# H3 sequence layer with a gated GLU, forward and backward: 128-channel key and value loads, a shorter sine table, and LN scaling and bf16 evacuations assigned to other engines

## The chip, the cores and the metric

One core of a Trainium2 chip. The metric is the device time of one execution in microseconds (us); runs are told by their median. The engines are named as the profile names them: PE multiplies matrices and transposes through them, DVE and ACT are the vector and the scalar engine, which also copy ("evacuate") PE's results from PSUM to SBUF, POOL issues one DMA queue and does small work, SP only issues DMAs (its own queue, in order).

## The reference

S = 2048 tokens, D = 512 channels, F = 1376, everything bf16. The kernel computes the output of the layer and, from `grad_out`, the gradients of nine of its inputs.

```
def _fwd_reference(A_q, A_k, A_v, A_shift_k, A_ssm_k, A_ssm_D, B_x, B_w_gate, B_w_up, B_w_down):
    xn = layernorm(A_q)
    k_shift = sum_t pad(A_k)[:, t:t+S] * A_shift_k[:, 3-t]      # four-tap causal convolution
    kv = k_shift * A_v
    y = irfft(rfft(kv, 2S) * rfft(A_ssm_k, 2S))[:, :S] + kv * A_ssm_D
    s = xn * y
    h = sigmoid(xn @ B_w_gate) * (xn @ B_w_up)
    return A_q + s * silu(h @ B_w_down)
# and the vector-Jacobian product with grad_out for q, k, v, shift_k, ssm_k, ssm_D, w_gate, w_up, w_down
```

## The kernel before

Nothing is emitted as it is written. Every `nc.<engine>.<op>` call is recorded by `Rec`, `Rec.order` (lines 348 to 504) gives each record a place by a list schedule with modelled costs (`cost`, `dcost`), and `emit` (line 506) issues the instructions in that order, which is why each instruction of the profile carries line 512. Each engine then runs its own list strictly in that order and waits on semaphores. An evacuation written as `nc.evac` (line 237) may go to ACT or DVE; the planner chooses (lines 414 to 420). So a changed cost or a changed program order moves instructions on all engines, but the order is fixed when the program is built.

The work has two stages around the change.

*FFT stage* (lines 766 to 1055, about the first 155 us). Four generators are merged by `run_streams` (line 1053):

- `strG` takes nine token tiles of 128 through `f_gen` (line 719): LN of a tile (`f_ln`, `f_ln2`: statistics on DVE, the power on POOL, then the scaling), its transpose (`f_xt`: PE with an evacuation, or a DMA transpose for some tiles), 88 matmuls with the gate and up weights, a sigmoid on ACT and a product on DVE (called `hT` below) for each of three blocks, and stores of `hT` and the sigmoid.
- `strV` does the four-tap convolution of the key with `A_shift_k` and the product with the value on DVE, per group of 128 channels (`GW`): eight TENSOR_TENSOR of 128x2048, 32 in all, and then the first FFT step on PE. Its loads are `ld_k` and `ld_v`, 256 channels each, so two groups share one load. The result of the convolution goes to DRAM (`ksh_d`) and its buffer `acc` is single.
- `strK` transforms the filter `A_ssm_k`: transposes (`k_t`), first step, then per quarter `flip` (eight PE transposes, a bf16 evacuation of 1024) and `step3` (f32 evacuation of 1024). Two SP DMAs swap the halves of each result (`slab<-slab`, 128 KB).
- `strX` flips and transforms the value side, multiplies both and goes back (`inv3`, `inv1`).

The FFT runs as matmuls with a sine table `Cf`, made at the start by `gen_fft_consts` (line 542): in four parts, integer products, masks to 13 bits, and one ACT sine of 1024 for cosine and sine together. The program order at the start is the loads of lines 812 to 824 on SP (filter, two token tiles, weights in three chunks, then key and value), the shift-filter broadcast `skb`, `k_t(0)`, and then the table with LN pieces between its yields (lines 850 to 860).

*Second stage* (line 1410 on): GLU down projection, all backward parts. Its instructions come after those of the FFT stage on each engine and need the results of that stage.

Transposes, flips and `k_t` write bf16 PSUM tiles; steps 1 and 3 and the inverse steps write f32 ones.

Of the kernel before, what the change touches and what calls it, by code (L numbers as in the profile page):

```python
# [16 lines left out]
P = 128  # L17
# [6 lines left out]
NJ = 16  # L24
# [132 lines left out]
class Op:  # L157
    __slots__ = ("n", "alts", "deps", "succ", "wait", "ready", "dma", "tiles", "done", "fin", "eng", "soft")

# [11 lines left out]
class Rec:  # L171
# [65 lines left out]
    def evac(self, dst, src, n):  # L237
        self.add([("scalar", "copy", (dst, src), {}), ("vector", "tensor_copy", (dst, src), {})])

# [48 lines left out]
    def cost(self, alt):  # L288

        eng, meth, a, k = alt  # L290
        out = k["out"] if "out" in k else a[0]
        n = self.size(out)
        if eng == "tensor":
            c = max(n, 128) / 2400 + 0.0025
            if out.ap.ap[0][1] <= 32 and len(out.ap.ap) > 2:
                c = 0.024
            return c, c + 0.163
        aps = [v for v in list(a) + list(k.values()) if isinstance(v, (PT, bass.AP))]
        big = [v for v in aps if self.size(v) >= n / 2]
        if eng == "scalar":  # L300
            ins = [v for v in big if v is not out]
            c = 0.045 + n * 0.84e-3
            if not any(isinstance(v, PT) for v in ins):
                c += 0.06 + (0.33e-3 * n if any(esize(v.dtype) == 4 for v in ins) else 0.0)
            return c, c + 0.11
        if eng == "vector":
            ps = any(isinstance(v, PT) for v in big)
            wide = any(esize(v.ap.dtype if isinstance(v, PT) else v.dtype) == 4 for v in big)
            rate, more = 960, 0.0
            if meth in ("tensor_copy", "tensor_scalar", "tensor_single_scalar", "tensor_scalar_add", "memset"):  # L310
                rate = 1920 if (wide and not ps) or (ps and not wide) else 960 if ps else 3840
                more = 0.11 if meth == "tensor_scalar" and n > 1000 else 0.0
            elif meth == "tensor_tensor" and not ps and not wide:
                rate = 1920
            if meth == "transpose":
                rate = 480
            if meth == "bn_stats":
                n, more = self.size(a[1]), 0.06
            elif meth == "scalar_tensor_tensor" and n > 100:
                more = 0.14  # L320
            c = 0.068 + n / rate + more
            return c, c + 0.085
        if "alu" in meth or meth == "tensor_tensor":
            return max(0.55, 0.2 + n * 2.1e-3), max(0.6, 0.25 + n * 2.1e-3)
        return 0.1 + n / 1000, 0.2 + n / 1000
# [22 lines left out]
    def order(self):  # L348
# [55 lines left out]
        while ndone < len(ops):  # L404
            best = None
            for e in self.ENGS:
# [135 lines left out]
def gen_fft_consts(nc, ar, negpi, Cf, TB):  # L542
    nc.vector.memset(negpi, -math.pi)
    sc = 2 * math.pi / 8192
# [9 lines left out]
    nc.gpsimd.iota(b, pattern=[[2, 128]], base=1, channel_multiplier=0)  # L554
    m = tmp([16, 128], i32)
    mc = tmp([2, 16, 128], i32)
# [54 lines left out]
    tri = tmp([5, 128], f32)  # L611
    nc.scalar.activation(tri, an, ACT.Sin, bias=negpi, scale=2 * math.pi / 16)
    nc.vector.tensor_tensor(TB[:, 0], tri[:, 0], mask[:, 0], ALU.mult)
# [11 lines left out]
def kernel_impl(ctx, tc, A_q, A_k, A_v, A_shift_k, A_ssm_k, A_ssm_D, B_x, B_w_gate, B_w_up, B_w_down,  # L625
# [29 lines left out]
    ident = Ring(ar, [P]).ap  # L655
    negpi = Ring(ar, [1], f32).ap
    TB = Ring(ar, [5, 128]).ap
# [133 lines left out]
    def ld_k(cp):  # L791
        c0, c1 = cp * 256, (cp + 1) * 256
        kh = kh_r.next()
# [5 lines left out]
    def ld_v(cp):  # L799
        vg = vg_r.next()  # L800
        nc.sync.dma_start(vg, vC[:, :, cp * 256:(cp + 1) * 256])
        stA["vg", cp] = vg
# [45 lines left out]
    for _ in k_t(0):  # L848
        pass
    consts = gen_fft_consts(nc, ar, negpi, Cf, TB)  # L850
    next(consts)
# [137 lines left out]
    def strV():  # L989
        for cg in range(NG):  # L990
            kh, vg = stA["kh", cg // 2], stA["vg", cg // 2]
            lc = (cg % 2) * GW
            c0, c1 = cg * GW, (cg + 1) * GW
            acc = acc_r.next()
            for lag in (3, 2, 1, 0):
                src = kh[:, 3 - lag: 3 - lag + NJ, lc:lc + GW]
                skl = skb[:, lag:lag + 1, c0:c1].to_broadcast([P, NJ, GW])
# [523 lines left out]
```

## Time and profile before

| what | value |
|---|---|
| median of 5 runs | 529.74 us (528.41 to 535.64) |
| the profiled execution: its own time | 530.13 us |
| its span, first to last instruction | 528.4 us |
| PE busy | 494.5 us, 94% of the span |
| DVE busy | 403.5 us, 76% |
| ACT busy | 342.5 us, 65% |
| POOL busy | 124.2 us, 24% |
| DMA moved | 113.19 MB, 214 GB/s on average |

Part 2 of the page cuts the span into 40 slices of 13.2 us and gives the busy share of each engine as one digit, so the FFT stage is the first twelve digits. The table of stretches gives, for a stretch of time, each engine's busy microseconds with the number of instructions in brackets, then the granted PE clock, the busy share of the DMA engines and the rate in GB/s. The groups by form name output, input, shapes and types, then the count, the busy sum and the mean ns of one instruction, then the idle time just before them and who ended it. The timeline lists instructions in order: start, duration, engine, operation, and in square brackets the idle time before it with the engine that ended it.

### The profile page before, as it was taken

Reading aid. Unit: us, or ns where it says so; the run is one execution under the profiler, and the core shown is the slowest. Engines: PE = TensorE matmul, PEld = TensorE weight load, DVE = VectorE, ACT = ScalarE, POOL = GpSimd, SP = SyncE. Lnnn points to the kernel's source line nnn. Section 1 sums busy time; section 2 is a strip of 40 time slices with the busy share of each in tenths; the row PEclk is TensorE's granted clock in tenths of the full one; section 3 lists DMA queues with packets and bytes.
Section 4 is the critical chain, followed back from the end, with each engine's and each line's share of the span. In section 5 each row is a group of like instructions: output and inputs, shape, how many; then the busy total and the mean of one; then the engine's idle time right before and its main releaser. Section 6 shows DMA issues by size and latency. Waiting matters only on the chain.

```text
span 528.4 us, 13550 instructions
## 1 busy us (share of the span) xinstructions
PE 494.5 (94%) x5429; PEld 349.4 (66%) x5429; DVE 403.5 (76%) x777; ACT 342.5 (65%) x455; POOL 124.2 (24%) x241
## 2 busy tenths in 40 slices
PE   4697899999999999999999999999999999998996
PEld 2686787898887676577775556644676755765643
DVE  7859999975749989978789999636758678773744
ACT  6899999999874345344443443326879968776621
POOL 5152533444513413424153221010000000000000
PEclk9899999999999999999999999999999999999999
DMA  8977796878999755647399946989898889999983
GB/s 258 258 226 267 240 336 203 265 238 244 225 197 216 165 154 147 207 118 194 109 253 244 205 137 176 224 249 255 188 255 220 204 261 213 253 182 241 210 213 117
DMA packets 173713, 113.19 MB, mean 214 GB/s; under 512 B 114487, under 2 KB 158161, under 8 KB 173394
## 3 DMA queue, kind: packets, MB, share of 16 engines
q1 hardware_dynamic: 162016, 78.43, 62.2%
q0 software_dynamic: 11104, 33.89, 21.0%
q8 instruction: 42, 0.69, 0.6%
q14 instruction: 21, 0.17, 0.1%
q10 hardware_dynamic: 530, 0.01, 0.1%
HBM read 37.65 MB, written 45.72 MB: 158 GB/s over the span
## 4 chain that ended last, share of the span: by engine, by line
PE 51%; DVE 21%; ACT 10%; issue 8%; DMA 6%; POOL 3%; DVEq 0%; POOLq 0%; ACTq 0%
PE psum L512 51%; DVE slab L512 21%; ACT slab L512 10%; DMA ksh_d<-slab 2%; DMA slab<-in_A_q_dram 1%; DMA KK_d<-slab 1%; DMA out_dram<-slab 1%; POOL slab L512 1%; POOL hF_d L512 1%; DMA Ci_d<-slab 1%; POOL KK_d L512 1%; POOL ksh_d L512 0%; POOL sF_d L512 0%; DVEq L512 0%; POOLq L512 0%
## 5 line engine op out<-in xcount | busy, mean ns | idle before, releaser
L512 PE MATMUL psum<-slab 128*128 128x128 bf16 (+4 forms) x5429 | 494.5, 255 | 29.0 <-ACT slab L512 17.1
L512 PEld LDWEIGHTS <-slab 128*128 128x128 bf16 (+2 forms) x5429 | 349.4, 99 | 173.8 <-issue 24.2
L512 DVE TENSOR_TENSOR slab<-slab 128x512 bf16<-128x512 bf16 (+6 forms) x472 | 268.6, 608 | 48.3 <-ACT slab L512 24.5
L512 ACT CAST slab<-psum 128x1024 bf16<-128x1024 f32 (+3 forms) x270 | 219.5, 861 | 98.2 <-PE psum L512 70.8
L512 ACT ACTIVATE slab<-psum 128x512 bf16<-128x512 f32 (+2 forms) x80 | 55.5, 694 | 45.5 <-PE psum L512 43.0
L512 ACT ACTIVATE slab<-slab 128x512 bf16<-128x512 bf16 (+2 forms) x53 | 42.1, 799 | 22.1 <-DVE slab L512 21.5
L512 ACT COPY slab<-psum 128x1024 bf16<-128x1024 bf16 (+1 forms) x49 | 46.9, 998 | 13.9 <-PE psum L512 13.9
L512 POOL DMA_DIRECT2D out_dram<-slab x32 | 17.5, 545 | 102.9 <-DVE slab L512 102.9
L512 DVE CAST slab<-psum 128x1024 bf16<-128x1024 f32 (+2 forms) x24 | 27.0, 1126 | 16.5 <-PE psum L512 13.8
L512 DVE TENSOR_TENSOR slab<-psum,slab 128x512 bf16<-128x512 f32 (+2 forms) x47 | 29.3, 626 | 11.9 <-ACT slab L512 7.2
L512 DVE SCALAR_TENSOR_TENSOR slab<-slab 128x512 bf16<-128x512 bf16 (+2 forms) x64 | 28.1, 439 | 7.9 <-POOL slab L512 5.7
L512 POOL DMA_DIRECT2D hF_d<-slab x48 | 26.0, 545 | 31.4 <-DVE slab L512 31.2
L512 POOL MEMSET slab<- 128x128 bf16 (+3 forms) x11 | 4.3, 400 | 118.0 <-PE psum L512 117.6
L512 DVE SCALAR_TENSOR_TENSOR slab<-psum,slab 128x512 bf16<-128x512 f32 x16 | 11.0, 688 | 21.0 <-PE psum L512 21.0
L512 POOL DMA_DIRECT2D KK_d<-slab x32 | 17.5, 546 | 21.7 <-ACT slab L512 18.5
L512 POOL DMA_DIRECT2D slab<-in_A_q_dram x29 | 16.2, 557 | 24.1 <-ACT slab L512 18.7
L512 DVE TENSOR_SCALAR slab<-slab 128x1 f32<-128x1 f32 (+9 forms) x54 | 16.4, 324 | 2.2 <-ACT slab L512 1.2
L512 DVE STREAM_TRANSPOSE slab<-slab 128x1024 f32<-128x1024 f32 x8 | 14.3, 1826 | 4.3 <-ACT slab L512 4.3
L512 POOL DMA_DIRECT2D slab<-hF_d x18 | 9.7, 542 | 10.8 <-PE psum L512 10.0
L512 DVE BATCH_NORM_STATS2 slab<-slab 128x6 f32<-128x512 bf16 x16 | 11.0, 687 | 1.4 <-DMA slab<-in_A_q_dram 1.4
L512 POOL TENSOR_TENSOR slab<-slab 128x1 f32<-128x1 f32 x16 | 9.8, 613 | 9.5 <-DVE slab L512 9.3
L512 POOL DMA_DIRECT2D slab<-in_grad_out_dram x16 | 8.6, 540 | 6.0 <-DMA out_dram<-slab 4.6
(20 smaller groups left out, 32.8 us busy)
## 6 DMA issues: line engine op xcount, KB each, us to landing
KK_d<-slab POOLq DMA_DIRECT2D x32, 256.0 KB, 4.3
slab<-KK_d SPq DMA_DIRECT2D x16, 512.0 KB, 4.4
slab<-in_A_v_dram SPq DMA_DIRECT2D x4, 1024.0 KB, 9.4
hF_d<-slab POOLq DMA_DIRECT2D x32, 128.0 KB, 3.8
slab<-slab SPq DMA_DIRECT2D x32, 128.0 KB, 4.7
out_dram<-slab POOLq DMA_DIRECT2D x32, 128.0 KB, 2.7
uF_d<-slab SPq DMA_DIRECT2D x32, 128.0 KB, 2.3
gF_d<-slab SPq DMA_DIRECT2D x32, 128.0 KB, 2.3
```

Of the source, the lines that this page charges most:

```text
L512: getattr(getattr(self.nc, eng), meth)(*[place(v) for v in a], **{x: place(v) for x, v in k.items()})
```

## The change

Key and value are loaded per 128 channels (eight loads each way instead of four, buffers of half the size, two of each), the first group ahead of the weights on SP's queue; the second group and the filter's second part are loaded at the end of the start-up. Of the table's four integer products three go to POOL; the two masks and an add become one shift pair and an absolute value (`-1 * x max x`), and cosine and sine are two ACT sines of 512 each. In the FFT stage LN's scaling is one DVE instruction with two per-partition scalars instead of a DVE product and an ACT instruction. The transposes of tiles 2 and 3 in the sequence go through PE instead of DMA. In the planner, evacuations of 2-byte PSUM tiles carry a bias of 0.3 us towards DVE, and the cost of 4-byte SBUF operations on DVE is set higher.

```
     def evac(self, dst, src, n):
-        self.add([("scalar", "copy", (dst, src), {}), ("vector", "tensor_copy", (dst, src), {})])
+        op = self.add([("scalar", "copy", (dst, src), {}), ("vector", "tensor_copy", (dst, src), {})])
+        op.bias = 0.3 if esize(src.ap.dtype) == 2 else 0
...
-                rate = 1920 if (wide and not ps) or (ps and not wide) else 960 if ps else 3840
+                rate = 1200 if wide and not ps else 1920 if ps and not wide else 960 if ps else 3840
...
-                    o = min(either, key=lambda o: (max(o.ready, free[e]), o.n))
+                    sg = 1.0 if e == "scalar" else -1.0
+                    o = min(either, key=lambda o: (max(o.ready, free[e]) + sg * o.bias, o.n))
                     s = (max(o.ready, free[e]), o.n, e, 1)
-                    late = free["scalar"] - s[0]
+                    late = free["scalar"] - s[0] + o.bias
...
+    nc.vector.memset(negpi[:, 1:2], math.pi / 2)
...
+    yield
+    m = tmp([4, 4, 128], i32)
+    mc = tmp([4, 2, 4, 128], i32)
+    for h in range(4):
+        eng = nc.gpsimd if h > 0 else nc.vector
+        eng.tensor_tensor(out=m[:, h], in0=a[:, 4 * h:4 * h + 4, None].to_broadcast([P, 4, 128]),
+                          in1=b[:, None, :].to_broadcast([P, 4, 128]), op=ALU.mult)
     for h in range(4):
         js = slice(4 * h, 4 * h + 4)
-        if h in (1, 2):
+        if h > 1:
             yield
-        nc.vector.tensor_tensor(m[:, js], a[:, js, None].to_broadcast([P, 4, 128]),
-                                b[:, None, :].to_broadcast([P, 4, 128]), ALU.mult)
-        nc.vector.tensor_single_scalar(mc[:, 0, js], m[:, js], 6144, ALU.add)
-        nc.vector.tensor_single_scalar(mc[:, 0, js], mc[:, 0, js], 8191, ALU.bitwise_and)
-        nc.vector.tensor_single_scalar(mc[:, 1, js], m[:, js], 8191, ALU.bitwise_and)
-        nc.scalar.activation(Cf[:, :, js], mc[:, :, js], ACT.Sin, bias=negpi, scale=sc)
+        nc.vector.tensor_scalar(mc[:, h, 1], m[:, h], 19, 19, ALU.logical_shift_left, ALU.arith_shift_right)
+        nc.scalar.activation(Cf[:, 1, js], mc[:, h, 1], ACT.Sin, scale=-sc)
+        nc.vector.scalar_tensor_tensor(mc[:, h, 0], mc[:, h, 1], -1, mc[:, h, 1], ALU.mult, ALU.max)
+        nc.scalar.activation(Cf[:, 0, js], mc[:, h, 0], ACT.Sin, bias=negpi[:, 1:2], scale=-sc)
...
     def f_ln2(i):
         xj, st = T[i]["xq"], T[i]["st"]
+        if PS["wide"]:
+            nc.vector.tensor_scalar(xnA[:, i, :], xj, st[:, 6:7], rstd_all[:, i:i + 1], ALU.subtract, ALU.mult)
+            return
...
     def f_xt(i):
-        if POS[i] > 1 and not 8 < POS[i] < 12:
+        if POS[i] > 3 and not 8 < POS[i] < 12:
...
-    kh_r = Ring(ar, [NJ + 3, 2 * GW])
-    vg_r = Ring(ar, [NJ, 2 * GW])
+    kh_r = Ring(ar, [NJ + 3, GW], n=2)
+    vg_r = Ring(ar, [NJ, GW], n=2)
...
     def ld_k(cp):
-        c0, c1 = cp * 256, (cp + 1) * 256
+        c0, c1 = cp * GW, (cp + 1) * GW
...
+    ld_k(0)
+    ld_v(0)
     ld_w(0, 512)
     ld_x(SEQ[2])
     ld_w(512, 1024)
     ld_w(1024, F)
-    ld_k(0)
-    ld_v(0)
...
+    consts = gen_fft_consts(nc, ar, negpi, Cf, TB)
+    next(consts)
     make_identity(nc, ident)
...
-    consts = gen_fft_consts(nc, ar, negpi, Cf, TB)
     next(consts)
     f_ln(SEQ[0])
     next(consts)
     f_xt(SEQ[0])
     f_ln(SEQ[1])
     next(consts)
+    ld_KT(1)
+    ld_k(1)
+    ld_v(1)
...
-            if cg + 1 < NG:
+            if 0 < cg < NG - 1:
                 ld_KT(cg + 1)
...
             kvt = kvt_r.next()
-            nc.vector.tensor_tensor(kvt, acc, vg[:, :, lc:lc + GW], ALU.mult)
-            if cg == 1:
-                ld_k(1)
-                ld_v(1)
+            nc.vector.tensor_tensor(kvt, acc, vg, ALU.mult)
+            if cg + 2 < NG:
+                ld_k(cg + 2)
+                ld_v(cg + 2)
```

More of the change, by code (lines that the diff above doesn't have):

```diff
@@ L157 @@
 class Op:
-    __slots__ = ("n", "alts", "deps", "succ", "wait", "ready", "dma", "tiles", "done", "fin", "eng", "soft")
+    __slots__ = ("n", "alts", "deps", "succ", "wait", "ready", "dma", "tiles", "done", "fin", "eng", "soft", "bias")
 class EngRec:
@@ L542, in gen_fft_consts @@
 def gen_fft_consts(nc, ar, negpi, Cf, TB):
-    nc.vector.memset(negpi, -math.pi)
+    nc.vector.memset(negpi[:, 0:1], -math.pi)
+    nc.vector.memset(negpi[:, 1:2], math.pi / 2)
     sc = 2 * math.pi / 8192
@@ L554, in gen_fft_consts @@
     nc.gpsimd.iota(b, pattern=[[2, 128]], base=1, channel_multiplier=0)
-    m = tmp([16, 128], i32)
-    mc = tmp([2, 16, 128], i32)
+    yield
[5 more added lines that the diff above has]
+                          in1=b[:, None, :].to_broadcast([P, 4, 128]), op=ALU.mult)
     for h in range(4):
         js = slice(4 * h, 4 * h + 4)
-        if h in (1, 2):
+        if h > 1:
             yield
-        nc.vector.tensor_tensor(m[:, js], a[:, js, None].to_broadcast([P, 4, 128]),
-                                b[:, None, :].to_broadcast([P, 4, 128]), ALU.mult)
-        nc.vector.tensor_single_scalar(mc[:, 0, js], m[:, js], 6144, ALU.add)
-        nc.vector.tensor_single_scalar(mc[:, 0, js], mc[:, 0, js], 8191, ALU.bitwise_and)
-        nc.vector.tensor_single_scalar(mc[:, 1, js], m[:, js], 8191, ALU.bitwise_and)
-        nc.scalar.activation(Cf[:, :, js], mc[:, :, js], ACT.Sin, bias=negpi, scale=sc)
+        nc.vector.tensor_scalar(mc[:, h, 1], m[:, h], 19, 19, ALU.logical_shift_left, ALU.arith_shift_right)
+        nc.scalar.activation(Cf[:, 1, js], mc[:, h, 1], ACT.Sin, scale=-sc)
+        nc.vector.scalar_tensor_tensor(mc[:, h, 0], mc[:, h, 1], -1, mc[:, h, 1], ALU.mult, ALU.max)
+        nc.scalar.activation(Cf[:, 0, js], mc[:, h, 0], ACT.Sin, bias=negpi[:, 1:2], scale=-sc)
     yield
@@ L611, in gen_fft_consts @@
     tri = tmp([5, 128], f32)
-    nc.scalar.activation(tri, an, ACT.Sin, bias=negpi, scale=2 * math.pi / 16)
+    nc.scalar.activation(tri, an, ACT.Sin, bias=negpi[:, 0:1], scale=2 * math.pi / 16)
     nc.vector.tensor_tensor(TB[:, 0], tri[:, 0], mask[:, 0], ALU.mult)
@@ L655, in kernel_impl @@
     ident = Ring(ar, [P]).ap
-    negpi = Ring(ar, [1], f32).ap
+    negpi = Ring(ar, [2], f32).ap
     TB = Ring(ar, [5, 128]).ap
@@ L800, in ld_v @@
         vg = vg_r.next()
-        nc.sync.dma_start(vg, vC[:, :, cp * 256:(cp + 1) * 256])
+        nc.sync.dma_start(vg, vC[:, :, cp * GW:(cp + 1) * GW])
         stA["vg", cp] = vg
@@ L990, in strV @@
         for cg in range(NG):
-            kh, vg = stA["kh", cg // 2], stA["vg", cg // 2]
-            lc = (cg % 2) * GW
+            kh, vg = stA["kh", cg], stA["vg", cg]
             c0, c1 = cg * GW, (cg + 1) * GW
@@ L995, in strV @@
             for lag in (3, 2, 1, 0):
-                src = kh[:, 3 - lag: 3 - lag + NJ, lc:lc + GW]
+                src = kh[:, 3 - lag: 3 - lag + NJ]
                 skl = skb[:, lag:lag + 1, c0:c1].to_broadcast([P, NJ, GW])
```

## The prediction, made before the changed kernel ran

> **What bounds the kernel now.** I read the busy shares in slices first, to find the stage where PE isn't full.
>
> ```profile
> PE   4697899999999999999999999999999999998996
> DVE  7859999975749989978789999636758678773744
> ACT  6899999999874345344443443326879968776621
> ```
>
> After the twelfth slice PE is at 9 nearly throughout. In slices 3 to 10 ACT is at 9, and DVE nearly so in 4 to 8. The built order of the changed kernel ends, on every engine, with the same long run of instructions as before (on PE the last 6995 rows, on DVE 540, on ACT 284), so all that is new lies in the FFT stage. The stretches cut it at the first and the last instruction of the convolution, and at 158.5 us, where PE's long unbroken run starts:
>
> ```profile
> 0.00:34.70 34.70, 22.35 (x277) 18.98 (x278) 22.90 (x72) 28.28 (x35) 14.96 (x35) 0.95 0.87 254
> 34.70:104.75 70.05, 61.86 (x923) 54.01 (x921) 65.92 (x89) 69.81 (x84) 27.75 (x50) 1.00 0.83 257
> 104.75:158.50 53.75, 52.06 (x809) 46.90 (x805) 33.41 (x62) 48.93 (x65) 21.82 (x43) 1.00 0.98 227
> 158.50:528.40 369.90, 358.26 (x3428) 229.53 (x3427) 281.26 (x558) 195.53 (x274) 59.71 (x113) 1.00 0.82 200
> ```
>
> Columns: length, then PE, weight loads, DVE, ACT, POOL, clock, DMA share, GB/s. In the second stretch ACT is busy 69.81 of 70.05 us and DVE 65.92: two full engines, PE waits on them. In the third PE is full (52.06 of 53.75). So the stage has a start, a DVE/ACT stretch and a PE stretch. What ends the start is seen in the timeline:
>
> ```profile
> 15.04 5.49 PE L512 MATMUL psum<-slab 128*128 128x128 bf16 x66 [2.32 <-ACT slab L512]
> 34.11 0.69 DVE L512 TENSOR_TENSOR slab<-psum,slab 128x512 bf16<-128x512 f32 x1 [1.62 <-ACT slab L512]
> 34.72 9.90 DVE L512 TENSOR_TENSOR slab<-slab 128x2048 bf16<-128x2048 bf16 x8
> ```
>
> The convolution stands on DVE behind five hT products, and the fifth, at 34.11, waited for a sigmoid on a full ACT. The same five products stand ahead of it in the new order.
>
> **The change, part by part.** Durations come from the groups by form:
>
> ```profile
> L512 ACT COPY slab<-psum 128x1024 bf16<-128x1024 bf16 x39 | 41.2, 1102 | 1.4 <-PE psum L512 1.4
> L512 ACT ACTIVATE slab<-slab 128x512 bf16<-128x512 bf16 x48 | 36.9, 771 | 19.3 <-DVE slab L512 18.7
> L512 ACT ACTIVATE slab<-slab 128x1024 bf16<-128x1024 int32 x4 | 4.5, 1140 | 2.6 <-DVE slab L512 2.6
> L512 DVE COPY slab<-psum 128x1024 bf16<-128x1024 bf16 x5 | 3.4, 688 | 1.5 <-ACT slab L512 0.8 <-PE psum L512 0.7
> L512 DVE CAST slab<-psum 128x1024 bf16<-128x1024 f32 x20 | 24.4, 1221 | 10.2 <-PE psum L512 7.5 <-DMA out_dram<-slab 2.1 <-ACT slab L512 0.4
> L512 DVE TENSOR_SCALAR slab<-slab 128x512 int32<-128x512 int32 x12 | 5.8, 515 | 1.4 <-ACT slab L512 1.2
> L512 DVE TENSOR_SCALAR slab<-slab 128x1408 bf16<-128x1408 bf16 x9 | 4.7, 523 | 0.1
> L512 DVE TENSOR_TENSOR slab<-slab 128x512 int32<-128x512 int32 x4 | 2.7, 683 | 1.3 <-POOL slab L512 1.3
> L512 DVE SCALAR_TENSOR_TENSOR slab<-slab 128x1 f32<-128x1 f32 x16 | 2.5, 154 | 5.7 <-POOL slab L512 5.7
> ```
>
> On ACT consecutive instructions overlap: in the timeline a 1024 evacuation starts 0.90 us after the one before it and an LN scaling holds the engine 0.72 (sigmoids 0.49 for 512, 0.38 for 384), so I count those spacings, row by row in the built order where I give ACT's work up to a point.
>
> *LN scaling, 11 tiles.* ACT loses 11 x 0.72 = 7.9 us. DVE gets 11 instructions of 512 in bf16. None is in the trace. Nearest is TENSOR_SCALAR 128x1408, 523 ns; with 128x1 at 154 ns the slope gives 154 + 512 x 0.262 = 288 ns. The upper end is the rate of BN_STATS on 512, 687 ns. I take 0.29: 3.2 us, less 11 x 0.154 = 1.7 for the product that goes, +1.5 (up to +5.9). DVE waited for POOL's power before, at that product, so no wait is new.
>
> *Evacuations.* By the built order eight bf16 ones of 1024 move from ACT to DVE, three f32 ones come back, and DVE has two more of 512, as tiles 2 and 3 now go through PE. ACT: -8 x 0.90 + 3 x 0.90 = -4.5. DVE: 8 x 0.688 - 3 x 1.221 + 2 x 0.425 = +2.7. PE gets eight transposes, 8 x 0.064 = 0.5 (the rate of its run of 192 in 12.26 us). SP loses two DMA transposes of about 1.3 us each.
>
> *Table.* DVE: 4 x 0.683 + 12 x 0.515 = 8.9 becomes 0.683 + 4 x 0.515 + 4 x 0.70 (the absolute value has two int32 inputs, as the product) = 5.5. ACT: one table load less (1.28), but eight sines of 512; 640 takes 828 ns and 1024 takes 1140, so 512 takes 724 by their slope, and 0.62 in spacing: 8 x 0.62 - 4 x 1.02 = +0.9.
>
> *Three products on POOL.* No row of before is near: POOL's 128x1 power takes 0.61 us, the lower end. The Trainium skill ("GPSIMD Engine Reference", 3.1 and 4.1) speaks against the move: it prices a two-input elementwise instruction at about 2.6 cycles an element at 1.2 GHz, an estimate of 1.1 us for 512, and advises VectorE. Twice that is my upper end. I take 1.1, 3.3 in all, from about 2.5 to 6 us. POOL's iotas stand behind, and DVE's small mask chain needs them only after 13 us; the first power before came at 10.15. With 2.2 each POOL would be free at 9, still in time. Hidden.
>
> *Loads.* Before the weights stand now 1.05 MB more. At the first stretch's 254 GB/s that is 4.1 us. The runs are 256 bytes instead of 512. These rows bear on it:
>
> ```profile
> slab<-in_A_ssm_k_dram SPq DMA_DIRECT2D x4, 512.0 KB, 6.1
> slab<-in_A_k_dram SPq DMA_DIRECT2D x2, 1024.0 KB, 9.3
> slab<-in_A_k_dram SPq DMA_DIRECT2D x4, 512.0 KB, 6.6
> ```
>
> The last line is this load, as the backward part already makes it: 0.5 us more than the filter, which has long runs and the same size. The Trainium skill ("DMA: Bandwidth & Descriptors", Specifications) says that transfers under 512 bytes miss line rate; if that halved it, 512 KB would land like 1024 KB, 2.7 us later, +5.4 for the pair ahead of the weights, and 8 x 2.7 = 22 over the stage. By the row it is +1.0 for the pair and 4 in all, on queues with a share of 0.83. I take the row. The last weights landed at 15.4 us (issued 6.84, 8.5 to landing); they will at 20.5 (rule: 25).
>
> *The start, summed.* The filter lands as before, so DVE reaches its k_t addition at 8.31. From there it has, ahead of the first token transpose's evacuation (now its own): two sets of LN statistics, 2 x (0.687 + 0.180 + 0.154) = 2.0; the last table part, 1.2; two scalings, 0.6; the mask chain, 3.2 between 15.04 and 18.2 in the trace, and tiny ones, 1.2; the evacuation, 0.4. That makes 16.9, so the gate matmuls start 2 us later than at 15.04. But the sines end near 15.3 (k_t's evacuations end at 11.56, then six x 0.62) instead of 18.4, so the 32 filter matmuls no longer share that run, and ACT has before the fifth sigmoid 17.5 us of work instead of 27.7, since flips, LN scalings and a table load went behind or away. PE then has 176 matmuls until the fifth hT: 176 x 0.064 = 11.3, to 28.2. With the product and latencies the convolution starts at 29.6 instead of 34.7: -5.1. Bounds: PE at the start's colder rate, 66 in 5.49 us, gives 31.6 plus 1.4, -1.7; no queueing behind the mask chain gives 26.5, -8.
>
> *The stretch.* In the new order DVE has between first and last convolution instruction 6 bf16 evacuations more, 3 f32 fewer, one statistics set fewer, one hT more, and 4 scalings for 4 products: 4.1 - 3.7 - 1.0 + 0.7 + 0.5 = +0.6. So DVE needs 65.9 + 0.6 = 66.5. ACT's work up to that point falls from 97.1 to 87.3, of which 66.7 are behind the start. PE has then done 1180 matmuls, 1172 before; about 950 fall in here, 950 x 0.067 = 63.7. Three engines near 65 don't interlock without loss; of 70.05 I take off 1.0 (0 to 3.5). DVE is the bound next, not ACT.
>
> *After it.* PE has the same work left and is full: 53.75, plus 0.5 for the transposes counted at the whole stage. Then the old list.
>
> Sum: -5.1 - 1.0 + 0.1 (the part of the transposes outside waits) = -6.0. The profiled execution took 530.13 us, 1.7 beside its span of 528.4, and would take 524.1. It is 0.39 above the median of the runs, 529.74, so I predict 523.7.
>
> **The rivals.**
>
> *ACT alone was the bound.* Its row of nines speaks for it. It sheds 7.9 + 4.5 + 1.28 - 0.9 = 12.8 us and the stage shrinks by 12: 517.7. Against it: DVE's 65.92 in the stretch doesn't shrink.
>
> *The gain is lost.* DVE's queue at the start decides: gate matmuls wait for an evacuation behind the mask chain, weights come later, and a cold PE starts the convolution near 34; the stretch stays at 70. Then -1: 529.
>
> *Slower, through SP's queue.* Groups 2 and 3 are loaded singly, each only once a convolution frees its buffer, and SP stands still meanwhile, with the half-swaps of the filter's transforms behind it. Before, the one such load held SP for 7.34 us (from 55.11). Two of them held so, each passed on whole to the products that stand on DVE among the convolution, cost 14.7: 529.74 - 6.0 + 14.7 = 538.4. It decides once SP is held longer than the swaps lead their products. Early this lead is some 20 us (30.4 to 53.4); against it too, DVE waited on swaps nowhere in this stage.
>
> **How the numbers follow.** Likeliest, -6: 0.52, own range 518 to 527. ACT alone: 0.20. Lost: 0.14. Slower: 0.14. About 1%, 5.3 us, is what a measurement of this kernel can tell, so faster means below 524.4: two thirds of the first case and all of the second, 0.56; same 0.30, the rest of the first and the third; slower 0.14. The range leaves out the slow case and the best end of the second: 514 to 531.
>
> **What would show it.** Right: first convolution instruction near 29.6, first sigmoid near 18 (20.72 before), the convolution's last end near 98.6, ACT below 97% in the stretch, PE's unbroken run starting near 152.5, scalings near 0.29 us. Wrong: a convolution start at 34 or later, a stretch over 71, DVE waits on `slab<-slab` or `in_A_k_dram` of microseconds, POOL products over 2.2 us, or a third stretch that keeps PE waiting on DMA, whose share there is already 0.98.

## The result and the profile after

The changed kernel takes 529.80 us (median of 44 runs), the kernel before 529.45 (79 runs): ratio 0.9993, 95% interval 0.9977 to 1.0009. The ratio leaves out the executions that lie over 1.5% above the fastest of their kernel (11 of the 44, two of them at 856 and 1799 us), so it is not the quotient of the two medians. The forecast was 523.7. The profiled execution of the changed kernel took 531.28 us, with a span of 529.5.

The slices first (PE, DVE, ACT, busy share in tenths):

```profile
PE   3889899999997999999999999999999999999996
DVE  8889989686758679978789999645758768883844
ACT  6689999788963344334443353234888968786621
```

PE is at 8 or 9 from the second slice on (before, from the fifth), and has a 7 in the thirteenth that was not there before. The stretches, cut at the same times as before (the last one is 0.6 us longer):

```profile
0.00:34.70 34.70, 23.81 (x287) 20.80 (x288) 28.99 (x72) 23.40 (x33) 20.27 (x41) 1.00 0.93 246
34.70:104.75 70.05, 63.57 (x937) 56.45 (x936) 63.79 (x86) 66.56 (x78) 28.69 (x49) 0.98 0.86 263
104.75:158.50 53.75, 53.49 (x819) 47.72 (x817) 37.51 (x70) 46.74 (x63) 22.38 (x44) 1.00 0.98 227
158.50:529.00 370.50, 356.85 (x3402) 227.85 (x3400) 278.66 (x552) 194.00 (x270) 59.03 (x112) 0.99 0.82 199
```

ACT has five nines in the first twelve slices, where it had eight: 23.40 us of work in the first stretch instead of 28.28, 66.56 in the second instead of 69.81. PE did more than before in each of the first three stretches (140.9 us up to 158.5, before 136.3), but in the last one it has 356.85 us of work where it had 358.26 in a shorter stretch, and the clock is 0.99 instead of 1.00. The timeline of the start shows where the convolution went (DVE; the fifth hT product, a product of one column between, then the convolution):

```profile
30.24 0.69 DVE L514 TENSOR_TENSOR slab<-psum,slab 128x512 bf16<-128x512 f32 x1 [0.20 <-PE psum L514]
30.85 6.13 DVE L514 TENSOR_TENSOR slab<-slab 128x2048 bf16<-128x2048 bf16 x5
```

It starts at 30.85 instead of 34.72, -3.9. I call the stage's end the first gate product of the second stage on DVE, which needs everything of the FFT stage behind it on PE: 156.32 before, 153.31 now, -3.0.

```profile
156.32 0.69 DVE L512 TENSOR_TENSOR slab<-psum,slab 128x512 bf16<-128x512 f32 x1 [3.14 <-ACT slab L512]
153.31 0.69 DVE L514 TENSOR_TENSOR slab<-psum,slab 128x512 bf16<-128x512 f32 x1 [3.45 <-ACT slab L514]
```

So the stage did become shorter. The work moved as it was built to: the groups by form, ACT's bf16 evacuations (39 before) and LN scalings (48 with those of the backward part), DVE's evacuations (5 bf16, 20 f32 before) and the new scalings.

```profile
L514 ACT COPY slab<-psum 128x1024 bf16<-128x1024 bf16 x31 | 33.2, 1108 | 4.3 <-PE psum L514 4.1
L514 ACT ACTIVATE slab<-slab 128x512 bf16<-128x512 bf16 x37 | 27.1, 735 | 19.2 <-DVE slab L514 18.7
L514 DVE CAST slab<-psum 128x1024 bf16<-128x1024 f32 x17 | 20.8, 1221 | 9.9 <-PE psum L514 8.6 <-ACT slab L514 1.1
L514 DVE COPY slab<-psum 128x1024 bf16<-128x1024 bf16 x13 | 8.8, 686 | 0.7 <-PE psum L514 0.5
L514 DVE TENSOR_SCALAR slab<-slab 128x512 bf16<-128x512 bf16 x11 | 5.6, 507 | 1.8 <-POOL slab L514 1.6
```

From the stage's end on, every engine has the list of before, and the gain is gone within 23 us. The timelines of PE, first the kernel before (from 160 us), then the changed one (from 150 us):

```profile
159.70 30.47 PE L512 MATMUL psum<-slab 128*128 128x512 bf16 x325
```

```profile
149.75 15.90 PE L514 MATMUL psum<-slab 128*128 128x512 bf16 x204
169.28 10.92 PE L514 MATMUL psum<-slab 128*128 128x512 bf16 x87 [3.63 <-DVE slab L514]
```

Before, PE ran on without a gap. Now it stands still for 3.63 us from 165.65, ahead of the input gradient of tile 0 (`x_gen(0)`: 11 matmuls of `duT` with the transposed up weights `wuT`, then 11 of `dgT` with `wgT`). DVE reads the sum at 175.81; before it did so at 173.85. A gain of 3.0 has become a loss of 2.0.

```profile
173.85 0.68 DVE L512 SCALAR_TENSOR_TENSOR slab<-psum,slab 128x512 bf16<-128x512 f32 x1
175.81 0.69 DVE L514 SCALAR_TENSOR_TENSOR slab<-psum,slab 128x512 bf16<-128x512 f32 x1 [4.89 <-PE psum L514]
```

The bracket names DVE, but DVE was through with its run of 16 products at 167.8, and in the kernel before PE passed this point while DVE was still in the same run (before first, then changed):

```profile
163.81 6.95 DVE L512 TENSOR_TENSOR slab<-slab 128x512 bf16<-128x512 bf16 x16
160.80 6.96 DVE L514 TENSOR_TENSOR slab<-slab 128x512 bf16<-128x512 bf16 x16
```

Each of the first eleven matmuls reads `wuT` over all its columns, so it needs all four transposes of the up weights, which SP issues last of twelve weight transposes. The view of these, in a window with the last two of the four, first before, then changed:

```profile
L512 SPq DMA_TRANSPOSE slab<-in_B_w_up_dram x2: 1802/2142/2483, 160.0 to 162.6; - x2
DMA to landing us min/median/max: 4.6/5.1/5.5
```

```profile
L514 SPq DMA_TRANSPOSE slab<-in_B_w_up_dram x2: 2241/2292/2342, 157.6 to 159.9; - x2
DMA to landing us min/median/max: 9.2/9.2/9.2
```

In the changed kernel the last was issued at 159.9 and landed 9.2 later, at 169.1: PE starts at 169.28. Before, the last of the four was issued at 162.6 and landed 4.6 later, at 167.2, and PE, which comes to this point 12.34 us after the stage's end, would have been there at 168.7. By this sum the kernel before had 1.5 us to spare. The changed kernel needed the weights 3 us sooner and got them 2 us later.

Behind the wait, the windows show the price of the second kind (columns as above):

```profile
164.00:170.00 6.00, 2.37 (x15) 0.97 (x13) 5.93 (x14) 0.69 (x2) 1.61 (x3) 0.93 1.14 144
170.00:176.00 6.00, 6.00 (x23) 2.44 (x22) 1.04 (x4) 0.00 (x0) 2.14 (x4) 0.79 0.97 232
```

23 matmuls fill 6 us, with a granted clock of 0.79; the first ones take 0.43 us each where 0.21 is usual. From PE's start to the reading of the sum it takes 6.5 us; it takes 4.9 where the clock stays at 1.00 (e4 and e14 below). The Trainium skill ("TensorE: Matmul & The Clock Gate", Part 1) says that TensorE falls to half rate after an idle window of some 3.4 us; the wait of 3.63 us and the doubled spacing agree with it here.

### The profile page after: what moved, and what is told of

It is laid out like the page before. It is cut to its first block, busy times and chain, and to the rows that moved or that the text cites. A ratio compares the mean times of both kernels' runs of the same rounds, so it can differ in the third digit from the quotient of the medians.

```text
span 529.5 us, 13557 instructions
## 1 busy us (share of the span) xinstructions
PE 497.7 (94%) x5437; PEld 352.8 (67%) x5437; DVE 409.0 (77%) x778; ACT 330.7 (62%) x442; POOL 130.4 (25%) x246
## 4 chain that ended last, share of the span: by engine, by line
PE 58%; DVE 21%; ACT 10%; issue 5%; DMA 3%; POOL 2%; DVEq 0%; POOLq 0%; ACTq 0%
PE psum L514 58%; DVE slab L514 21%; ACT slab L514 10%; DMA slab<-in_A_q_dram 1%; DMA hF_d<-slab 1%; POOL slab L514 1%; DMA KK_d<-slab 1%; POOL hF_d L514 0%; POOL KK_d L514 0%; POOL sF_d L514 0%; DVEq L514 0%; POOL ksh_d L514 0%; POOLq L514 0%; ACTq L514 0%; POOLq L1517 0%
## 5 line engine op out<-in xcount | busy, mean ns | idle before, releaser
L514 DVE TENSOR_TENSOR slab<-slab 128x512 bf16<-128x512 bf16 (+5 forms) x469 | 267.0, 608 | 42.8 <-ACT slab L514 26.3
L514 ACT CAST slab<-psum 128x1024 bf16<-128x1024 f32 (+4 forms) x273 | 220.8, 861 | 102.4 <-PE psum L514 77.2
L514 ACT COPY slab<-psum 128x1024 bf16<-128x1024 bf16 (+1 forms) x41 | 38.7, 993 | 15.8 <-PE psum L514 15.6
L514 ACT ACTIVATE slab<-slab 128x512 bf16<-128x512 bf16 (+2 forms) x46 | 32.8, 727 | 22.4 <-DVE slab L514 21.9
L514 DVE CAST slab<-psum 128x1024 bf16<-128x1024 f32 (+2 forms) x21 | 23.4, 1112 | 16.2 <-PE psum L514 15.0
L514 POOL MEMSET slab<- 1x384 bf16 (+2 forms) x13 | 4.5, 352 | 120.3 <-PE psum L514 119.5
L514 DVE SCALAR_TENSOR_TENSOR slab<-slab 128x512 bf16<-128x512 bf16 (+3 forms) x57 | 30.6, 536 | 3.0 <-ACT slab L514 1.1
L514 DVE TENSOR_SCALAR slab<-slab 128x1 f32<-128x1 f32 (+10 forms) x57 | 19.1, 350 | 2.6 <-POOL slab L514 1.6
L514 POOL TENSOR_TENSOR slab<-slab 128x1 f32<-128x1 f32 (+1 forms) x19 | 15.7, 831 | 12.9 <-DVE slab L514 12.6
L514 DVE COPY slab<-psum 128x1024 bf16<-128x1024 bf16 (+1 forms) x16 | 9.9, 636 | 1.4 <-PE psum L514 1.2
```

The source lines that it names most:

```text
L514: getattr(getattr(self.nc, eng), meth)(*[place(v) for v in a], **{x: place(v) for x, v in k.items()})
```

## The experiments

Main theory: the FFT stage gained what the trace shows, and PE then waits for the up-weight transposes, whose arrival lay 1.5 us beneath the old end. First rival: DVE, which the profile names, is late. Second rival: the loss is a lower clock all over the run and the wait a side effect.

All ratios are to the kernel before, in runs on the same chip. The marks are from the one profiled execution of each kernel.

| kernel | ratio, interval | convolution starts | stage ends | PE waits at tile 0's input gradient | its sum is read |
|---|---|---|---|---|---|
| before | 1 | 34.72 | 156.32 | none | 173.85 |
| changed | 0.9993, 0.9977 to 1.0009 | 30.85 | 153.31 | 3.63 | 175.81 |
| e1 gate half first | 0.9969, 0.9940 to 0.9997 | 30.50 | 151.90 | 1.58 | 170.77 |
| e2 plain up loads | 0.9938, 0.9909 to 0.9967 | 30.83 | 156.97 | none | 174.50 |
| e3 before, plain up loads | 0.9984, 0.9961 to 1.0007 | 34.81 | 156.41 | none | 173.94 |
| e4 filled wait | 1.0007, 0.9972 to 1.0042 | 30.23 | 151.28 | 0.31 | 172.33 |
| e5 LN alone | 1.0168, 1.0092 to 1.0244 | 37.23 | 158.86 | none | 176.37 |
| e6 loads alone | 1.0017, 0.9990 to 1.0044 | 43.49 | 155.99 | 2.19 | 175.48 |
| e7 table alone | 1.0168, 1.0096 to 1.0239 | 34.68 | 160.85 | 2.87 | 181.01 |
| e8 evacuations alone | 1.0007, 0.9971 to 1.0042 | 35.22 | 155.67 | 1.14 | 174.10 |
| e9 gate transposes early | 1.0167, 1.0122 to 1.0212 | 31.68 | - | none | - |
| e10 before, the same | 1.0209, 1.0166 to 1.0253 | 34.73 | - | none | - |
| e11 products on DVE | 0.9944, 0.9926 to 0.9963 | 39.60 | 153.60 | none | 171.22 |
| e12 without LN part | 0.9989, 0.9960 to 1.0017 | 44.09 | 153.93 | 3.77 | 176.68 |
| e13 before, up twice | 1.0289, 1.0231 to 1.0348 | 34.63 | 155.18 | 19.00 | 193.71 |
| e14 changed, again | 0.9991, 0.9954 to 1.0027 | 30.25 | 151.23 | 1.97 | 170.50 |
| e15 e11 and gate half first | 0.9957, 0.9931 to 0.9983 | 39.35 | 153.35 | none | 170.97 |

Where the convolution starts after 39 us, the scheduler has put other DVE work ahead of it; that column can't be compared there. e1, e2, e4 and e14 leave the FFT stage of the changed kernel as it is. Three of them end it at 151.2 to 151.9, and e2, whose clock fell twice in the stage, at 156.97; so 153.31 is one execution of several, and a single mark is good to 2 us at best.

**The wait: e1 to e4.** The edits, shortened: in `x_gen` (e1), in the loop of the transposes (e2, and e3 on the kernel before; both leave the transposition of the up weights out), and at the place where the input gradient is issued (e4):

```
-        for srcT, wT in ((duT, wuT), (dgT, wgT)):
+        for srcT, wT in ((dgT, wgT), (duT, wuT)) if i == 0 else ((duT, wuT), (dgT, wgT)):
...
-            nc.sync.dma_start_transpose(w[:, 0:NFB - 1, ds], src[ds, 0:128 * (NFB - 1)])
+            if w is wuT: nc.sync.dma_start(w[:, 0:NFB - 1, ds], src[ds, 0:128 * (NFB - 1)].rearrange("d (b f) -> d b f", f=128))
+            else: nc.sync.dma_start_transpose(w[:, 0:NFB - 1, ds], src[ds, 0:128 * (NFB - 1)])
...
+                if op.n == self.fill[0]:      # the first matmul of x_gen(0)
+                    for _ in range(16): self.nc.tensor.matmul(psX, wd[:, 0, 0:128], wd[:, 0, :], start=True, stop=True)
```

> The changed kernel, with one edit: for tile 0 the input gradient takes the gate half first (dgT with wgT), then the up half. Main theory: the 3.0 us that the FFT stage gains are waited away at tile 0's input gradient, whose first matmul needs the last up-weight transpose, which lands at 169.15 us. With the gate half first this transpose is needed 11 matmuls x 0.215 = 2.4 us later, so of the wait of 3.63 us about 1.0 stays, too short for the clock to fall, and the 22 matmuls behind it take 4.7 us instead of 6.5: -2.6 - 1.8 = -4.4 us against the changed kernel, about 525.5 us, ratio to before 0.993. Rival 1 (VectorE, which the profile names as the releaser, is late with the products that these matmuls read): its last product comes no sooner, the wait stays above 3 us and the time at 529.5. Rival 2 (the loss is a lower granted clock spread over the whole run, the wait a side effect): the wait goes, the mean clock stays near 0.992, the time at 529.5.

> The changed kernel, with the four up-weight transposes for the backward part replaced by plain loads of the same bytes; this leaves the transposition out, so the input gradient is computed with wrongly laid out weights. Main theory: without the late transposes PE doesn't stop at tile 0's input gradient: -3.63 - 1.8 = -5.4 us against the changed kernel, 524.5 us, ratio to before 0.991. Rival 1 (VectorE late): the wait of some 3.6 us stays, 529.5. Rival 2 (clock spread over the run): no wait, but 529.5 at a mean clock of 0.992.

> The kernel before, with the same four transposes replaced by plain loads (transposition left out there too). Main theory: before, PE came to tile 0's input gradient just after the last transpose had landed and did not wait, so nothing is to be had: 529.5 us, ratio 1.000 within 0.002. If the transposes cost time by the traffic that they make and not by this wait, the ratio falls as in the changed kernel, to about 0.991.

> The changed kernel, with 16 more matmuls of 128x512 put ahead of tile 0's input gradient, on operands that are long there and into the bank that the next matmul overwrites: PE is busy through the wait instead of idle. Main theory with its second part (the idle wait halves the clock for the matmuls behind it): the input gradient still can't start before 169.2 us, but its 22 matmuls take 4.7 instead of 6.5 us: -1.8 us, 528.0, ratio to before 0.997. If the slow matmuls have another cause than the idle time, they stay at 0.43 us each and the time at 529.7.

In e1, PE does the gate half at once and waits in front of the up half, for 1.58 us:

```profile
149.82 16.80 PE L514 MATMUL psum<-slab 128*128 128x128 bf16 x200
168.20 22.11 PE L514 MATMUL psum<-slab 128*128 128x512 bf16 x247 [1.58 <-issue]
```

The clock stays at 1.00 behind it. The time falls, by less than I expected: 0.9969 against 0.993, with 1.58 us of wait left where I had reckoned 1.0. The landing fits here too: the last transpose lands at 168.1 (issued at 158.5, 9.6 to landing), PE starts on the up half at 168.20. The same holds in every other kernel of the table that waits here for a transpose (e4, e6, e7, e8, e12, e13, e14): PE starts 0.1 to 0.3 us after the last landing. In e2 the wait is gone:

```profile
149.79 40.41 PE L514 MATMUL psum<-slab 128*128 128x128 bf16 x446
```

and the time is 0.6% under before (0.9% was expected), although in this profiled execution the clock fell in the stage (0.58 from 148 to 152 us) and its end came 3.7 us later than in the changed kernel. The same edit is worth 0.55% on the changed kernel and 0.16% on the kernel before (e3, whose interval holds zero). DVE's instructions there are those of the changed kernel in e1 and e2, so the first rival is out. In its pure form the second is out too: without the wait the time fell.

e4 shows the clock: with PE busy through the wait, the same 22 matmuls run at full rate.

```profile
163.46 3.62 PE L516 MATMUL psum<-slab 128*128 128x512 bf16 x16
167.39 22.82 PE L517 MATMUL psum<-slab 128*128 128x512 bf16 x234 [0.31 <-DVE slab L517]
```

The sum is read 4.9 us after 167.39, so the slow matmuls came of the idle time. The other kernels agree: after waits of 1.14 to 2.87 us (e6, e7, e8, e14) the sum is read 4.9 to 5.0 us after PE's start, after waits of 3.63, 3.77 and 19.00 us (changed, e12, e13) 6.5 to 7.2 us after it. But the median did not fall (1.0007, where I expected 0.997). The halving is shown in these traces; that it is worth 1.8 us in the median is not. In e4's execution the rest of the run took 355.0 us from the sum on, 1.7 more than in e14; 1.0 of it is a longer wait for ACT at 482 us, and why it is longer is open.

**How near the second bound was: e13.** Each of the four transposes is issued twice, in the kernel before (shortened):

```
-                getattr(getattr(self.nc, eng), meth)(...)
+                for _ in range(2 if op.n in self.twice else 1): getattr(getattr(self.nc, eng), meth)(...)
```

> The kernel before, with each of the four up-weight transposes issued twice into the same place. They land some 8 to 9 us later. Main theory: the kernel before had about 1.5 us to spare there (last transpose issued at 162.6 us, landing 4.6 us later, input gradient of tile 0 near 168.7), so PE waits 6 to 8 us, its clock falls for the matmuls behind, and the time rises by 8 to 10 us: ratio 1.015 to 1.019. If before had much to spare, the ratio is 1.000 to 1.003.

```profile
186.53 13.78 PE L513 MATMUL psum<-slab 128*128 128x512 bf16 x118 [19.00 <-DMA slab<-in_B_w_up_dram]
```

Here the profile names the DMA. My size was off by a factor of two, since the copies went one behind another: SP's eight issues took 28.50 us where the four took 7.76. The last one landed at 186.4 (issued at 183.0, 3.4 to landing) instead of 167.2, 19.2 us later; in this execution PE came there 1.1 us sooner than in the kernel before (stage's end 155.18), and it waited 19.0. So before had 19.2 + 1.1 - 19.0 = 1.3 us to spare, near the 1.5 that its trace gave.

**The parts alone: e5 to e8, and e12.** These take the hunks of the change as they are: e5 the branch `if PS["wide"]` of `f_ln2`, e6 the buffers and calls of `ld_k`, `ld_v` and `ld_KT`, e7 `gen_fft_consts` with its earlier call and the changed cost, e8 `bias` with `POS[i] > 3`. e12 is the changed kernel without the branch of e5.

> The kernel before, with the LN scaling of the FFT stage on VectorE alone. By the steps of the prediction ScalarE loses 4 x 0.72 = 2.9 us ahead of the fifth sigmoid, so the convolution starts near 32 us (34.7 before), and the stage (read at the first gate product of the z stage, 156.3 before) ends 1 to 3 us sooner. Main theory: the time still stays within 0.3% of before, since tile 0's input gradient then waits for the up-weight transposes. Rival: what ScalarE sheds VectorE takes on, and both being full the stage ends no sooner than 156.

> The kernel before, with key and value by 128 channels in front of the weights alone. The first weights land some 4 us later, ScalarE has all its work of before ahead of the fifth sigmoid: the convolution starts at 35 to 37 us, no sooner than before, the stage ends at 156 or later, the time is 529.5 to 532. If instead the loads were what held the convolution before, it starts sooner than 33 here.

> The kernel before, with the shorter table generation alone (three products on GpSimd, shift pair, absolute value, sines by 512, generation begun ahead of the filter). By the steps of the prediction the sines end near 15.5 us instead of 18.4 and one table load goes: the convolution starts 2 to 3 us sooner, near 32, and the stage ends 1 to 2 us sooner. If VectorE's int32 work beside GpSimd's products (1.41 instead of 0.69 us for one) eats the saving, the convolution starts at 34 or later. The time within 0.3% of before in both cases.

> The kernel before, with the lean of bf16 evacuations to VectorE and tiles 2 and 3 transposed on TensorE alone. ScalarE -4.5 us over the stage, VectorE +2.7: the convolution starts up to 1.5 us sooner, and the stretch to its last instruction, where VectorE has 4 us to spare, shortens by 1 to 2; the stage ends near 154.5, the time within 0.3% of before. Rival: TensorE waits longer for VectorE in the stretch than it gains from ScalarE, and the stage ends at 156 or later.

> The changed kernel, with the LN scaling of the FFT stage back on ScalarE (the other three parts stay). Alone on the kernel before, the LN part put the stage's end from 156.3 to 158.9 us. If the parts add up, taking it out ends the stage sooner, near 151. If they need each other (ScalarE has room only with the table and the evacuations shortened, VectorE likewise), it ends later, at 155 to 158, with ScalarE full again from 35 to 100 us; the time is then 529 to 533.

None of the parts ends the stage more than 0.7 us sooner by itself; I had expected 1 to 3 us from e5, 1 to 2 from e7 and about 2 from e8. Their shifts are +2.5, -0.3, +4.5 and -0.7, together about +6; all four at once gave -3.0 in one execution and -5.1 in another (e14). With marks that scatter so, -0.3 and -0.7 are not told from nothing, and a part of e7's +4.5 may be its clock (0.68 and 0.89 from 44 to 52 us); but +6 against -3 to -5 is more than that. Taking LN out of the four (e12) ends the stage at 153.93, 0.6 us behind the changed kernel and 2.7 behind e14, neither the 151 nor the 155 to 158 that I had written down. The parts don't add up. e5 shows one reason, and refutes the rival *ACT alone* of the prediction. The stretch up to 158.5 us in e5, then ACT's timeline around its first sigmoid:

```profile
0.00:158.50 158.50, 135.98 (x1960) 119.95 (x1961) 127.89 (x223) 132.02 (x159) 64.44 (x128) 1.00 0.87 243
```

```profile
20.37 0.83 ACT L512 ACTIVATE slab<-slab 128x640 f32<-128x640 int32 x1 [2.55 <-DVE slab L512]
21.22 1.28 ACT L512 ACT_TABLE_LOAD   x1
22.51 0.60 ACT L512 ACTIVATE slab<-psum 128x512 bf16<-128x512 f32 x1
```

ACT is busy 15 us less than before (132.0, it was 147.0; up to each kernel's stage end 132.4 and 145.1, as the planner also moved eight evacuations to DVE), and the stage ends 2.5 us later. What ACT gave up stands on DVE in front of the mask chain, the last sine waits 2.55 us for that, and the first sigmoid comes at 22.51 instead of 20.72. That the shorter table makes the room for it on DVE is my reading; no run has these two parts alone. e5 and e7 also lost 1.7% of time (few executions, five and four). In e7 the marks tell it (the sum is read 7.2 us later). In e5 they tell 2.5 of 9 us, and its profiled execution, 529.58 us, was the quickest of its five; the rest of its loss is open.

**An early place for the gate transposes: e9 and e10.** The list is changed after scheduling:

```
+        late = [x for x in seq if x[0].n in self.early]     # the gate-weight transposes
+        seq = [x for x in seq if x[0].n not in self.early]
+        at = 1 + max(n for n, x in enumerate(seq) if x[0].n in self.behind)    # the loads of wd
+        seq[at:at] = late
```

> The changed kernel, with the four gate-weight transposes moved up on SP's queue, ahead of the last filter half-swaps, to where the DMA share is 0.44 (their release token is taken from an earlier filter product); nothing else changes its place. Main theory: eight transposes are then left for the stretch from 127 us on, the last up-weight transpose lands near 160 instead of 169, and PE reaches tile 0's input gradient at about 165.5 without waiting: -3.6 - 1.8 = -5.4 us against the changed kernel, a ratio to before of 0.990 to 0.994 (524.5 to 526.5 us). If the gain of the stage is lost elsewhere, the wait goes and the time stays at 529.5; if the half-swaps behind the moved transposes come too late, the stage ends later than 154 and the time is 529 or more.

> The kernel before with the same move of the four gate-weight transposes. Main theory: there PE did not wait for them, so there is little to be had, ratio 0.997 to 1.001 (the plain loads of the up weights gave 0.9984). If the move helps by easing DMA traffic in general, the ratio is as low as in the changed kernel, 0.994 or less.

A miss of the design: `wgT` lies where filter data still had its readers, and these, now behind the transposes, read gate weights, so the filter's spectrum and the gradients that need it are not the reference's. PE waited for the transposes in the middle of the stage:

```profile
PE psum L518 <- DMA slab<-in_B_w_gate_dram: 10.4, 4, 7.4
```

(us in total, times, longest.) It tells that the transposes can't start that early in this layout, and nothing on the theory.

**The products back on DVE: e11, e15; the changed kernel again: e14.**

```
-        eng = nc.gpsimd if h > 0 else nc.vector
+        eng = nc.vector
```

> The changed kernel, with the three table products back on VectorE. VectorE gets 3 x 0.68 = 2.0 us of products, and its absolute values and one shift pair beside GpSimd's products (1.41, 1.41 and 1.26 us in the changed kernel against 0.69 and 0.52) become short again, -2.2: the start is the same within 0.5 us (convolution at 30.4 to 31.4) and the time within 0.3% of the changed kernel. If the move to GpSimd was worth its 2 us, the convolution starts near 33; if it cost, near 29.

> The changed kernel itself once more, unedited, on the chip of the next kernel. Main theory: 1.000 within 0.003 to before, with a wait of 2 to 4 us at tile 0's input gradient in its trace.

> The changed kernel with the three products back on VectorE and, for tile 0, the gate half first. Main theory: the products kernel no longer waited at tile 0's input gradient, so the order of the halves changes nothing: 0.994 to before within 0.003, 3 us under the changed kernel on the same chip. If the products kernel's lead was chance, it is at 0.997 to 1.000 like the others.

e11 is the best of the kernels that leave nothing out, for a reason that I had not written down. Its start is worse: the first sigmoid is at 24.00, 3.0 later than in the changed kernel, so the move to POOL, with the list that comes of it, is worth some 3 us there. Its stage ends at 153.60, like that of the changed kernel. But the weight transposes get through sooner. The first of them is issued at 128.71 (128.73 in the changed kernel); then three of the down weights take SP 8.25 us instead of 12.39. Why is not shown. SP's timeline, last transposes, e11:

```profile
144.89 6.73 SPq L514 DMA_TRANSPOSE slab<-in_B_w_gate_dram  x2
151.92 8.30 SPq L514 DMA_TRANSPOSE slab<-in_B_w_up_dram  x4
```

and the changed kernel:

```profile
148.60 5.05 SPq L514 DMA_TRANSPOSE slab<-in_B_w_gate_dram  x2
153.95 8.32 SPq L514 DMA_TRANSPOSE slab<-in_B_w_up_dram  x4
```

The last of e11 lands at 164.7 (issued at 158.6, 6.1 to landing), 1.2 us before PE comes there; PE does not wait, and the time is 0.9944. Two profiled executions with the same stage end, 153.3 and 153.6, differ by that wait and by the slow matmuls behind it: their sums are read 4.6 us apart, and the medians of the two kernels differ by half a per cent. e15 repeats it (0.9957), and there the gate half first adds nothing, as expected.

e14 is the changed kernel in an execution without a fall of the clock:

```profile
149.75 13.83 PE L514 MATMUL psum<-slab 128*128 128x512 bf16 x184
165.55 14.81 PE L514 MATMUL psum<-slab 128*128 128x512 bf16 x142 [1.97 <-DVE slab L514]
```

It reads the sum at 170.50, the first one at 175.81. The 5.3 us between two executions of one program are: the stage's end, 2.1 (151.23 against 153.31, where the first has clocks of 0.75 and 0.82 from 92 to 100 us), the wait, 1.7 (3.63 against 1.97), and the slow matmuls, 1.6. Beside the kernel before (173.85) e14 is still 3.4 us ahead at the sum: of the 5.1 us that its stage gained, 1.7 are lost here. That execution took 525.52 us, 3.4 less than the median of before on its chip; but the median of e14's own 14 executions is 529.55. So the wait alone doesn't account for a ratio of 1.

That also bears on the second rival. Of the executions that the comparison uses, the clock was at 0.999 or more in 6 of 44 of the changed kernel, in 47 of 159 of before, and in 26 of 42 of e11 and e15. The medians of the spans of these alone are 523.7, 525.9 and 524.8. So with a full clock the changed kernel is some 2 us faster than before, and it seldom has it. The lower clock is thus the likely second part of the loss. It may itself come in part of the wait (shortened or filled, in e1 and e4, the clock was full in 5 of 13 and 6 of 14); no run parts the two, and six executions are too few for a size.

## Why the prediction was wrong

- **The failed step is "After it. PE has the same work left and is full: 53.75 [...] Then the old list."** I took it that what follows moves with the stage's end. The list is the old one, but its input gradient waits for a DMA chain that did not move with it: the first weight transpose was issued at 128.73 (129.14 before), the last landed at 169.1 (167.2). The stage's end was the bound, and the next bound lay 1.3 to 1.5 us beneath it (e13 and the trace of before). PE waited 3.63 us there and took 1.6 us longer behind the wait. With the wait shortened (e1) or gone (e2) the time falls by 0.3 and 0.6%, not by the 1.1% that were forecast: in the undisturbed execution the wait takes 1.7 of 5.1 us, and what takes the rest in the median, the lower clock being the candidate, stays open. A DMA share of 0.98 stood in the row that I showed, and "a third stretch that keeps PE waiting on DMA" among the signs of being wrong; I gave it no rival and no price. The rival *the gain is lost* has the right number, 529, for the wrong reason: it let the convolution start at 34.
- **The stage itself.** In the undisturbed execution (e14) it ends 5.1 us sooner, forecast 6.0. The terms: the start -4.5 (forecast -5.1); the stretch +1.6 (71.62 us from the first to the end of the last convolution instruction, forecast -1.0); behind it -2.2 (49.36 us to the stage's end, before 51.57), where I had +0.1. I had called that stretch full, though PE idled 1.7 us in it. The sum was near, two terms were not.
- **DVE's work in the stretch** is 66.69 us in e14, forecast 66.5. ACT's is 69.43, forecast 66.7: the mis-sized term there. "DVE is the bound next, not ACT" was wrong too: ACT is still the busier one, 97% of 71.62 us against DVE's 93%. Why the stretch became longer is not shown.
- **The start.** The gate matmuls begin at 18.31 (forecast 16.9), the first sigmoid comes at 21.00 ("near 18"): the last sine waited 3.28 us for DVE's masks. The scalings take 0.40 us in the timeline where nothing interferes (507 ns in the mean of the group), not 0.29. The 0.29 was computed from a slope that a wider form of the same instruction gave; the measured times lie inside the bounds.
- **The table.** The groups by form:

```profile
L514 DVE SCALAR_TENSOR_TENSOR slab<-slab 128x512 int32<-128x512 int32 x4 | 4.2, 1046 | 0.1
L514 POOL TENSOR_TENSOR slab<-slab 128x512 int32<-128x512 int32 x3 | 3.8, 1306 | 0.0
L514 DVE TENSOR_SCALAR slab<-slab 128x512 int32<-128x512 int32 x4 | 3.0, 752 | 0.0
```

A POOL product takes 1.31 us (forecast 1.1, upper end 2.2). "Hidden" was not quite true: two absolute values beside the products took 1.41 us instead of 0.69, one shift pair 1.26. DVE spent 7.9 us on the table, not 5.5.
- **Loads.** The prediction weighed a row of before, 6.6 us for 512 KB, against the rule that it cites, some 9.3, and took the row. The profile's row for the eight loads of this form:

```profile
slab<-in_A_k_dram SPq DMA_DIRECT2D x8, 512.0 KB, 7.8
```

The four of the FFT stage took 8.3 in the median, between the two and nearer to the 9.3. It cost little: DVE never waited for them.
- **The slower rival, through SP's queue,** did not come: DVE had no wait for a half-swap or a load in the stage.

## What to carry to other kernels

Before pricing a stage's shortening, ask of everything behind it what else it waits for, and when that arrives. Transfers that start on their own trigger don't move along, and a wait of zero in the profile of before may be a slack of 1.5 us. Read it as arrival (issue plus landing) against need. Gains and costs of moving work between engines that interlock are not to be summed part by part, least of all where a scheduler lays out the list anew.

## What the hardware showed

- One program, two executions, 5.3 us apart by 175 us. In the first the granted clock was 0.50 from 94 to 97 us, behind 4 us in which PE was busy 2.41 us (23 matmuls, no gap over 0.64 us). In e14, 0.6 us earlier, PE had the same 4 us, 2.41 busy with 23 matmuls, and the clock stayed at 1.00. So the clock can fall without a long idle window, and the same work doesn't always make it fall.
- DVE's int32 instructions can slow down beside POOL's. In e11 a shift pair beside POOL's iotas took 2.49 us instead of 0.43:

```profile
4.08 2.49 DVE L514 TENSOR_SCALAR slab<-slab 128x512 int32<-128x512 int32 x1
```

The Trainium skill ("SBUF — State Buffer", Who interferes with whom) has the two engines share a port pair that one of them holds for a whole instruction, which agrees; I had not looked there for the price of "hidden".
- The up-weight transposes, all of one size, took 4.4 to 9.6 us from issue to landing (e11 and e1), with a DMA share of 0.97 or more in each 4 us from 152 to 164, and 3.4 in e13 with a share of 0.55.
